# Smallest score chunks first for the first pair, products of zeros ahead of it, and new durations and numbers in the plan of a mixer kernel

## The chip, the core and the metric

The kernel runs on one core of a Trainium2 chip. The metric is the device time in microseconds (us) of one execution, lower is better. Three runs of the kernel before took 779.51, 781.88 and 781.61 us; their median is 781.61 us. The trace read below is of one further, profiled execution.

## The reference

`B, H, S, D = 4, 12, 448, 64`, `DM = 768`. Causal attention per head is followed by a two-stage mixer (tokens, then channels) with residuals and by a gated block whose gate is mixed over tokens after a layer normalisation.

```python
scores = q @ k.T / 8, masked above the diagonal
attn = exp(scores - max) / (sum + 1e-9)
x = (attn @ v), heads joined                       # (4, 448, 768)
h = relu(x^T @ w_tok1) @ w_tok2                    # over tokens
u = x + h^T
x = u + relu(u @ w_ch1) @ w_ch2                    # over channels, 1536 wide
h = relu(x @ w_in); u, v = halves of h             # 512 each
v_n = (v - mean(v)) / sqrt(var(v) + 1e-6)
out = (u * (w_spatial @ v_n + b_spatial)) @ w_out
```

## The kernel before, in words

All of it is one program of four batches. Products that need full precision are made of three products of rounded parts: a value is split into a high part (a copy to the shorter type, by ACT) and a low part (value minus high part, `lo_part` at line 251, by DVE or POOL), and `mm3` (line 257) multiplies high by high, high by low and low by high.

**Attention.** 24 pairs of heads go through `scores` (line 360), `transposed` or `turned` (lines 460 and 505) and `weighted` (line 556). A pair's scores are computed in four chunks of query rows (64, 128, 128 and 128 rows against 64, 192, 320 and 448 keys), two heads side by side, into four PSUM banks. Pairs below `WHOLE` multiply the loaded values (tile `stage`) directly; later pairs are first split by `split_qk` (line 348; tiles `qh`, `ql`). DVE adds the mask and finds the row extreme (line 417), ACT takes the exponentials and their sums (line 434), DVE adds 1e-9 to the eight sums and inverts them (lines 442 and 443), POOL scales (line 451). Pairs below `BLOCKS` are transposed on PE in 16 blocks (line 488), copied out of PSUM (lines 492 and 494) and multiplied with the values `v` (lines 592 and 597). Later pairs are transposed by DVE (line 518) and through DRAM by SP's transfers, and multiplied at line 578. Pairs below `AHEAD` use four places for their scores, later ones two.

**Mixers.** `token_mix` works per half batch (tiles `xs`, `hid`, sums into `U` at line 695). `channel` (line 769) does batches 0 and 1 with weights `whl` (tiles `uhl`, `hid`, sums at line 767); `channel_pair` (line 947) does batches 2 and 3 together with seven products in place of eight (`factors` at line 802, `split_weights` at line 838, `seven` at line 915; PSUM tiles `psf`, operands `fb` and `fa`, sums at lines 908 and 987). Weights arrive in double precision and DVE narrows them in three operations (lines 276, 278 and 280: tiles `way` and `gw`).

**Gated block.** For batches 0 and 1 and then 2 and 3 the first half of the hidden channels is again made by seven products (`hidden_pair`, line 1158), the other half by `value` (line 1077): 18 products into `psv`, a ReLU by ACT into one of two buffers `v` (line 1096), statistics by DVE (`first`, lines 1099 to 1101), a square root by ACT (line 1104), and normalisation by DVE (`second`, lines 1108 to 1113, output `vn`). `spatial` (line 1253) multiplies with `w_spatial` (PSUM `psp`), DVE adds the bias (line 1269) and multiplies by the gate (line 1270). `out_factors` and `project` (lines 1195 and 1281) make the output.

**The order.** Nothing is issued as it is written. Each piece is a `job` with an engine, a duration in us, what it reads and writes, and a priority; `Plan.order` (line 126) runs a list schedule over all jobs with those durations, and the instructions of each engine are emitted in the order of the planned start times. Each engine then executes its list in order. Jobs marked `port` and all POOL jobs exclude each other in the plan. A PSUM bank is chosen in the plan as well: the one that came free last, where one is free. So a wrong duration puts work in an order, or a tile in a bank, that does not suit the real times. Lines that the steps below touch:

```python
job("DVE", 0.8, first, r=[(v, 0)], w=[st], prio=p0)                  # line 1103
job("DVE", 0.65, second, r=[st, (v, 0)], w=[st, dkey], prio=p0)      # line 1115
v = buf(f"p{turns[0] % 2}", [FF], F32, "v")                          # line 1088
s = max(s, min(bank_free[i] for i in b.banks))                       # line 154
```

Of the kernel before, what the change touches and what calls it, by code (L numbers as in the profile page):

```python
# [9 lines left out]
F32 = mybir.dt.float32  # L10
# [25 lines left out]

DIRECT = tuple(range(3))

WHOLE = 6

AHEAD = 11

EAGER, START, STEP = 12, 110.0, 16.7

LO_DVE = tuple(range(7))
WEIGHT_LO_DVE = tuple(range(7))

GATE_DVE = tuple(range(8))
OUT_DVE = tuple(range(7))

VALUE_DVE = ()
NORMED_DVE = (1, 2, 3)

EARLY = 1e5 + 48
VALUE_PRIO = -1e5 + 1.5

GATED = 6.0, 0.3
GATED_AT = 160.0, 5.0

MOVE = 0  # L60
WEIGHT_PRIO = -0.7

AHEAD_OF_USE = 9.0
LEAD, SLOPE = 14.0, 2.0

BLOCKS = 16


class Buf:
# [20 lines left out]
class Plan:  # L90
# [11 lines left out]
    def job(self, eng, us, emit, r=(), w=(), touch=(), prio=0.0, at=0.0, size=0, port=False):  # L102


        j = Job(eng, us, emit, prio, at, size, len(self.jobs), port)
        for k in r:
            if k in self.writer:
                j.before.add(self.writer[k])
            self.readers.setdefault(k, []).append(j)
        for k in w:  # L110
            if k in self.writer:
                j.before.add(self.writer[k])
            j.before.update(self.readers.get(k, ()))
            self.writer[k] = j
            self.readers[k] = []
        j.before.discard(j)
        for k in (*r, *w):
            if isinstance(k[0], Buf):
                j.bufs.add(k[0])
        for b in j.bufs:  # L120
            b.jobs.append(j)
        j.bufs |= set(touch)
        self.jobs.append(j)
        return j
# [79 lines left out]
def mixer_kernel(ctx: ExitStack, tc: tile.TileContext, qkv, wtok, wch, wgv, wsp, bsp, out):  # L204
# [126 lines left out]
    def load(n):  # L331
        st = stage[n % 2]
        operands[n] = {"st": st}
        p = n - 2.0
        src = qkv[n // NP, n % NP]
        job("SP", 0.4, lambda: nc.sync.dma_start(st.t, src[:, : 2 * S]), w=[(st, 0)], prio=p, size=458752)
        v = buf(f"v{n % 2}", [8, D], F32, "v")
        operands[n]["v"] = v
        job("SP", 0.4, lambda: nc.sync.dma_start(v.t, src[:, 2 * S :].rearrange("p (c d) -> p c d", d=D)), w=[(v, 0)], prio=p + 0.1, size=262144)

    def prio_of(n):

# [17 lines left out]
    def scores(n):  # L360
# [35 lines left out]
        def ps(i, j):  # L396
            k, o_ = PLACE[i]
            M, W = CHUNKS[i][1] - CHUNKS[i][0], CHUNKS[i][1]
            return banks[j][k].t[:M, o_ : o_ + W]

        def mms():
            for i in (3, 0, 2, 1):
                q0, q1 = CHUNKS[i]
                W = q1
                ks = [slice(2 * S - W, 2 * S) if n < BLOCKS else slice(S, S + W), slice(S, S + W)]
                for k, (a, c) in enumerate(terms):
                    for j in range(2):
                        r = slice(64 * j, 64 * j + 64)
                        nc.tensor.matmul(ps(i, j), a.t[r, q0:q1], c.t[r, ks[j]], start=(k == 0), stop=(k == last))  # L409

        pkeys = [(banks[j][k], 0) for j in range(2) for k in range(2)]
        job("PE", 2.5 if whole else 1.95, mms, r=split_keys, w=[*pkeys, ("scored", n)], touch=holds, prio=n, at=nominal(n))
        for i in (3, 0, 2, 1):
            M, W = CHUNKS[i][1] - CHUNKS[i][0], CHUNKS[i][1]
            for j in range(2):
                def ttr(i=i, j=j, M=M, W=W):
                    nc.vector.tensor_tensor_reduce(  # L417
                        out=P(i)[:M, j, :],
                        in0=ps(i, j),
                        in1=mask[:M, S - 128 : S - 128 + W] if j == 0 and n < BLOCKS or M == 64 else mask[:M, S - W : S],  # L420
                        scale=-1.0 / 8.0,
                        scalar=3.0e38,
                        op0=ALU.add,
                        op1=ALU.min,
                        accum_out=s.t[:M, 0, 2 * i + j : 2 * i + j + 1],
                    )

                job("DVE", (W * 1.06 + 65) / 1e3, ttr, r=[(banks[j][PLACE[i][0]], 0), MASK], w=[pk(i, j), (s, "nm", i, j)], prio=prio_of(n))
        for i in (3, 0, 2, 1):
            M, W = CHUNKS[i][1] - CHUNKS[i][0], CHUNKS[i][1]  # L430
            for j in range(2):
                def ex(i=i, j=j, M=M):
                    c = 2 * i + j
                    nc.scalar.activation(  # L434
                        P(i)[:M, j, :], P(i)[:M, j, :], AF.Exp, bias=s.t[:M, 0, c : c + 1], scale=-1.0, accum_out=s.t[:M, 1, c : c + 1]
                    )

                job("ACT", (W * 0.833 + 279) / 1e3, ex, r=[(s, "nm", i, j), pk(i, j)], w=[pk(i, j), (s, "sum", i, j)], prio=prio_of(n))
# [638 lines left out]
    def value(lhs, keys, key, dst, dkey):  # L1077
# [22 lines left out]
            nc.vector.bn_aggr(sc(6, 2), sc(0, 6))  # L1100
            nc.vector.tensor_scalar_add(sc(8), sc(7), LN_EPS)

        job("DVE", 0.8, first, r=[(v, 0)], w=[st], prio=p0)
        job("ACT", 0.25, lambda: nc.scalar.activation(sc(9), sc(8), AF.Sqrt), r=[st], w=[st], prio=p0)

        def second():
# [5 lines left out]
            nc.vector.tensor_scalar_mul(r, r, t)  # L1112
            nc.vector.tensor_scalar(dst(), v.t, sc(6), r, op0=ALU.subtract, op1=ALU.mult)

        job("DVE", 0.65, second, r=[st, (v, 0)], w=[st, dkey], prio=p0)
        normal[key] = dst, dkey

    def gate_unit(f):
# [198 lines left out]
    project(1, place, ws, (1, 2))  # L1317


    make_identity(nc, ident)  # L1320
    nc.gpsimd.memset(mask, 0.0)
    diag = mask[:, S - 128 : S]
# [2 lines left out]
    )  # L1325
    for s in stats:
        nc.gpsimd.memset(s.t, 0.0)
    for t in small:

        nc.gpsimd.memset(t.t[64:128, 384:512], 0.0)  # L1330
    for j in plan.order():
        j.emit()
    mctx.__exit__(None, None, None)
# [69 lines left out]
```

## Time and profile before

| | |
|---|---|
| median of three runs | 781.61 us |
| profiled execution, own time | 780.77 us |
| its span, first to last instruction | 779.0 us |
| PE busy | 747.1 us (96%) |
| DVE busy | 637.7 us (82%) |
| ACT busy | 432.7 us (56%) |
| POOL busy | 259.8 us (33%) |
| mean granted clock of TensorE | 0.989 |

PE is the engine with the most work, so the time is read as PE's work plus the stretches in which PE has nothing to do. A busy PE can still be slow: the granted clock of a stretch tells whether it ran at the higher or the lower of its two levels.

### The profile page before, as it was taken

Reading aid. Unit: us, or ns where it says so; the run is one execution under the profiler, and the core shown is the slowest. Engines: PE = TensorE matmul, PEld = TensorE weight load, DVE = VectorE, ACT = ScalarE, POOL = GpSimd, SP = SyncE. Lnnn points to the kernel's source line nnn. Section 1 sums busy time; section 2 is a strip of 40 time slices with the busy share of each in tenths; the row PEclk is TensorE's granted clock in tenths of the full one; section 3 lists DMA queues with packets and bytes.
Section 4 is the critical chain, followed back from the end, with each engine's and each line's share of the span. In section 5 each row is a group of like instructions: output and inputs, shape, how many; then the busy total and the mean of one; then the engine's idle time right before and its main releaser. Section 6 shows DMA issues by size and latency. Waiting matters only on the chain.

```text
span 779.0 us, 12423 instructions
## 1 busy us (share of the span) xinstructions
PE 747.1 (96%) x4200; PEld 640.8 (82%) x4200; DVE 637.7 (82%) x1528; ACT 432.7 (56%) x1049; POOL 259.8 (33%) x333
## 2 busy tenths in 40 slices
PE   6889899999999999999998999999998999989998
PEld 3467678888988788888887999998887888879997
DVE  5899878898877868787479879999999797689582
ACT  5999766644455665542345667454554655535241
POOL 4789646375856564652500000001310200200000
PEclk9999999999999999999999999999999999989999
DMA  7677585789857998988732212322301100300113
GB/s 263 212 241 245 196 310 201 233 293 315 282 174 229 298 300 251 279 254 259 200 122 111 68 56 82 130 93 82 96 0 41 41 1 18 112 0 36 72 48 130
DMA packets 49679, 124.11 MB, mean 159 GB/s; under 512 B 4944, under 2 KB 20944, under 8 KB 49104
## 3 DMA queue, kind: packets, MB, share of 16 engines
q1 hardware_dynamic: 49616, 123.33, 48.3%
q8 instruction: 33, 0.54, 0.3%
q14 instruction: 30, 0.25, 0.1%
HBM read 92.50 MB, written 30.80 MB: 158 GB/s over the span
## 4 chain that ended last, share of the span: by engine, by line
PE 61%; DVE 27%; ACT 6%; issue 3%; DMA 2%; POOL 1%; DVEq 0%; ACTq 0%; POOLq 0%; SPq 0%
PE ps L261 7%; PE ps L263 7%; PE ps L262 7%; DVE fb L252 6%; PE psf L261 5%; PE psf L263 5%; PE psf L262 5%; DVE fa L252 4%; PE pss L409 4%; DVE raw L859 3%; PE pst L488 3%; DVE U L987 2%; PE pso L578 2%; ACT P L434 2%; DVE U L815 2%
## 5 line engine op out<-in xcount | busy, mean ns | idle before, releaser
L261 PE MATMUL psf<-fb,fa 128*128 128x448 f32 x420 | 154.7, 368 | 4.4 <-DVE hs L908 1.6
L263 PE MATMUL psf<-fb,fa 128*128 128x448 f32 x420 | 154.0, 367 | 0.0
L262 PE MATMUL psf<-fb,fa 128*128 128x448 f32 x420 | 154.0, 367 | 0.0
L252 POOL TENSOR_TENSOR whl<-whl 128x768 fp32r<-128x768 f32 x45 | 83.5, 1859 | 88.3 <-ACT whl L727 80.2
L451 POOL TENSOR_SCALAR P<-P,stats 128x448 f32<-128x448 f32 (+1 forms) x192 | 88.0, 477 | 48.4 <-DVE stats L443 36.3
L434 ACT ACTIVATE P<-P,stats 128x448 f32<-128x448 f32 (+1 forms) x192 | 95.9, 506 | 10.9 <-DVE stats L417 10.7
L261 PEld LDWEIGHTS psf<-fb,fa 128*128 128x128 f32 x420 | 79.3, 189 | 13.4 <-issue 1.9
L262 PEld LDWEIGHTS psf<-fb,fa 128*128 128x128 f32 x420 | 79.3, 189 | 6.7
L263 PEld LDWEIGHTS psf<-fb,fa 128*128 128x128 f32 x420 | 79.2, 189 | 6.8 <-DVE fa L252 0.2
L417 DVE CUSTOM_DVE_ANT_0 P<-pss,mask 128x448 f32<-128x448 f32 (+1 forms) x192 | 68.8, 412 | 15.0 <-PE pss L409 14.9
L846 ACT CAST fa<-raw 128x384 fp32r<-128x384 f32 (+1 forms) x112 | 57.0, 531 | 41.4 <-DVE raw L859 18.4
L252 DVE TENSOR_TENSOR fa<-raw,fa 128x384 fp32r<-128x384 f32 (+1 forms) x112 | 65.5, 611 | 9.8 <-ACT fa L846 9.6
L727 ACT CAST whl<-whl 128x768 fp32r<-128x768 f32 x45 | 37.2, 832 | 52.1 <-DMA whl<-plain 50.5
L252 POOL TENSOR_TENSOR wv<-wf,wv 128x512 fp32r<-128x512 f32 x6 | 8.5, 1430 | 161.0 <-DVE fb L252 153.1
L261 PE MATMUL ps<-uhl,whl 128*128 128x448 f32 x144 | 55.2, 383 | 0.0
L261 PE MATMUL ps<-hid,whl 128*128 128x448 f32 x144 | 54.2, 377 | 0.6 <-DVE U L767 0.6
L263 PE MATMUL ps<-hid,whl 128*128 128x448 f32 x144 | 52.7, 366 | 0.0
L263 PE MATMUL ps<-uhl,whl 128*128 128x448 f32 x144 | 52.7, 366 | 0.0
L262 PE MATMUL ps<-hid,whl 128*128 128x448 f32 x144 | 52.7, 366 | 0.0
L262 PE MATMUL ps<-uhl,whl 128*128 128x448 f32 x144 | 52.6, 365 | 0.0
L810 ACT CAST fb<-U 128x448 fp32r<-128x448 f32 x57 | 30.2, 566 | 29.5 <-DVE U L815 12.2
L488 PE MATMUL pst<-ident,P 128*128 128x128 f32 x256 | 38.7, 287 | 5.7 <-POOL P L451 4.5
(163 smaller groups left out, 1772.9 us busy)
## 6 DMA issues: line engine op xcount, KB each, us to landing
way<-in_wch SPq DMA_DIRECT2D x24, 768.0 KB, 6.1
whl<-plain SPq DMA_DIRECT2D x45, 384.0 KB, 5.4
stage<-in_qkv SPq DMA_DIRECT2D x24, 448.0 KB, 4.3
plain<-way SPq DMA_DIRECT2D x24, 384.0 KB, 3.8
raw<-plain SPq DMA_DIRECT2D x24, 384.0 KB, 3.7
round<-PB SPq DMA_DIRECT2D x8, 1024.0 KB, 6.8
PT<-round SPq DMA_DIRECT2D x32, 256.0 KB, 7.1
v<-in_qkv SPq DMA_DIRECT2D x24, 256.0 KB, 4.5
```

The costliest lines, as they stand in the source:

```text
L252: e.tensor_tensor(lo, x, hi.bitcast(F32), op=ALU.subtract)
L261: nc.tensor.matmul(ps, ah, bh, start=(first and i == 0), stop=False, **kw)
L262: nc.tensor.matmul(ps, ah, bl, start=False, stop=False, **kw)
L263: nc.tensor.matmul(ps, al, bh, start=False, stop=(last and i == n - 1), **kw)
L409: nc.tensor.matmul(ps(i, j), a.t[r, q0:q1], c.t[r, ks[j]], start=(k == 0), stop=(k == last))
L417: nc.vector.tensor_tensor_reduce(out=P(i)[:M, j, :], in0=ps(i, j), in1=mask[:M, S - 128 : S - 128 + W] if j == 0 and n < BLOCKS or M == 64 ...
L434: nc.scalar.activation(P(i)[:M, j, :], P(i)[:M, j, :], AF.Exp, bias=s.t[:M, 0, c : c + 1], scale=-1.0, accum_out=s.t[:M, 1, c : c + 1])
L451: nc.gpsimd.tensor_scalar(P(i)[:M, j, :], P(i)[:M, j, :], s.t[:M, 2, c : c + 1], 1.0, op0=ALU.mult, op1=ALU.mult)
L488: nc.tensor.transpose(ps.t[:, c : c + 128], src, ident)
L727: job("ACT", act(DM, False), lambda: nc.scalar.copy(w.t[:, 0, :], w.t[:, 1, :].bitcast(F32)), r=ks, w=ks, prio=p)
L810: job("ACT", act(S, False), lambda: nc.scalar.copy(f(0), x_()), r=wk, w=[(h, k, 0)], prio=p)
L846: job("ACT", act(n, False), lambda: nc.scalar.copy(part(o, 0), at(d)), r=[key(d)], w=[wk], prio=p + 0.1 * o)
```

## The change

The first pair's chunks are computed and read in the order 64, 192, 320, 448 keys instead of 448, 64, 320, 192; its `v` is loaded after the second pair's `stage`. DVE clears a buffer first of all and PE multiplies zeros by zeros (448 and 256 columns) into a PSUM bank that nothing reads. The plan gets 1.0 and 1.45 us for the two DVE parts of a value's statistics. Besides, its numbers change: one more pair (number 6) multiplies unsplit (`WHOLE`), pair 10 uses two places instead of four (`AHEAD`), pair 16 is transposed on PE instead of DVE and DRAM (`BLOCKS`), the low parts of product 0 of the gated block go from DVE to POOL (`GATE_DVE`), the splits of the value weights `wv` get a late priority (`VALUE_PRIO`), and several start times and priorities move.

```diff
-WHOLE = 6
-AHEAD = 11
-EAGER, START, STEP = 12, 110.0, 16.7
+WHOLE = 7
+AHEAD = 10
+EAGER, START, STEP = 12, 105.0, 16.4
-GATE_DVE = tuple(range(8))
+GATE_DVE = (1, 2, 3, 4, 5, 6, 7)
-EARLY = 1e5 + 48
-VALUE_PRIO = -1e5 + 1.5
+EARLY = 1e5 + 40
+VALUE_PRIO = 100.0
-GATED_AT = 160.0, 5.0
+GATED_AT = 160.0, 7.0
-AHEAD_OF_USE = 9.0
-LEAD, SLOPE = 14.0, 2.0
-BLOCKS = 16
+AHEAD_OF_USE = 12.0
+LEAD, SLOPE = 12.0, 2.0
+BLOCKS = 17
...
-        job("SP", 0.4, lambda: nc.sync.dma_start(v.t, src[:, 2 * S :].rearrange("p (c d) -> p c d", d=D)), w=[(v, 0)], prio=p + 0.1, size=262144)
+        job("SP", 0.4, lambda: nc.sync.dma_start(v.t, src[:, 2 * S :].rearrange("p (c d) -> p c d", d=D)), w=[(v, 0)], prio=p + (0.1 if n else 1.1), size=262144)
...
+        chunks = (3, 0, 2, 1) if n else range(4)
+
         def mms():
-            for i in (3, 0, 2, 1):
+            for i in chunks:
...
-        for i in (3, 0, 2, 1):
+        for i in chunks:
...
-        job("DVE", 0.8, first, r=[(v, 0)], w=[st], prio=p0)
+        job("DVE", 1.0, first, r=[(v, 0)], w=[st], prio=p0)
...
-        job("DVE", 0.65, second, r=[st, (v, 0)], w=[st, dkey], prio=p0)
+        job("DVE", 1.45, second, r=[st, (v, 0)], w=[st, dkey], prio=p0)
...
+    nc.vector.memset(small[0].t, 0.0)
+    zeros = psp.tile([128, 512], F32, tag="b7", name="zeros")
+    for n in (S, 256):
+        nc.tensor.matmul(zeros[:, :n], small[0].t[:, :128], small[0].t[:, :n], start=True, stop=True)
...
-    for t in small:
-
-        nc.gpsimd.memset(t.t[64:128, 384:512], 0.0)
+
+    nc.gpsimd.memset(small[1].t[64:128, 384:512], 0.0)
```

How instructions move is shown at three places, all on DVE, whose list PE waits for there.

**Place A**, the end of the first pair's score chunks and its inversion of sums (`way_149` and `way_152` are the first token weights, `stats_65` holds the first pair's sums). Before, and then in the change:

```order
L417 ISA P_69,stats_65<-pss,mask 128x192
L417 ISA stats_65 128x1
L276 TENSOR_SCALAR psw<-way_149 128x384
L278 SCALAR_TENSOR_TENSOR psw<-way_149,psw 128x384
L280 SCALAR_TENSOR_TENSOR way_149<-way_149,psw 128x384
L442 TENSOR_SCALAR stats_65<-stats_65 128x8
L443 RECIPROCAL stats_65<-stats_65 128x8
```

```order
L419 ISA P_177,stats_65<-pss,mask 128x448
L419 ISA stats_65 128x1
L276 TENSOR_SCALAR psw<-way_152 128x384
L278 SCALAR_TENSOR_TENSOR psw<-way_152,psw 128x384
L280 SCALAR_TENSOR_TENSOR way_152<-way_152,psw 128x384
L444 TENSOR_SCALAR stats_65<-stats_65 128x8
L445 RECIPROCAL stats_65<-stats_65 128x8
```

The last chunk is now the one of 448 keys; the narrowing of the first weights still stands ahead of the inversion.

**Place B**, the statistics of the first values of batches 0 and 1 (`U_5599` and `U_5474` are the fetched activations that `factors` subtracts and splits). Before, and then in the change:

```order
L815 TENSOR_TENSOR U_5599<-U_5599 128x448
L1099 BN_STATS bias<-v 128x6
L1100 BN_AGGR bias<-bias 128x2
L1101 TENSOR_SCALAR bias<-bias 128x1
L1099 BN_STATS bias<-v 128x6
L1100 BN_AGGR bias<-bias 128x2
L1101 TENSOR_SCALAR bias<-bias 128x1
L1108 RECIPROCAL bias<-bias 128x1
L1110 TENSOR_SCALAR bias<-bias 128x1
L1111 TENSOR_SCALAR bias<-bias 128x1
L1112 TENSOR_SCALAR bias<-bias 128x1
L1113 TENSOR_SCALAR vn<-v,bias 128x512
```

```order
L989 TENSOR_TENSOR U_2484<-psf,U_2484 128x448
L1101 BN_STATS bias<-v 128x6
L1102 BN_AGGR bias<-bias 128x2
L1103 TENSOR_SCALAR bias<-bias 128x1
L252 TENSOR_TENSOR fb<-U_5474,fb 128x448
L817 TENSOR_TENSOR U_5444<-U_5444 128x448 x3
L252 TENSOR_TENSOR fb<-U_5444,fb 128x448 x2
L252 TENSOR_TENSOR fb<-U_5474,fb 128x448
L817 TENSOR_TENSOR U_5474<-U_5474 128x448
L252 TENSOR_TENSOR fb<-U_5444,fb 128x448
L252 TENSOR_TENSOR fb<-U_5474,fb 128x448 x2
L817 TENSOR_TENSOR U_5474<-U_5474 128x448
```

The first value's statistics stood behind nearly all subtractions and splits of `U`; now they stand right behind the last sum of the channel mixer, with some of those splits between their two parts.

**Place C**, the last value's statistics and the first bias additions of `spatial` (`fa<-raw` and `raw<-raw` are the output weights' splits and sums, `gate_6375` and `gate_6304` the gate of batch 0). Before, and then in the change:

```order
L252 TENSOR_TENSOR fa<-raw,fa 128x768
L1099 BN_STATS bias<-v 128x6
L1100 BN_AGGR bias<-bias 128x2
L1101 TENSOR_SCALAR bias<-bias 128x1
L252 TENSOR_TENSOR fa<-raw,fa 128x768
L1269 TENSOR_TENSOR psp<-psp,bias 128x448
L1108 RECIPROCAL bias<-bias 128x1
L1110 TENSOR_SCALAR bias<-bias 128x1
L1111 TENSOR_SCALAR bias<-bias 128x1
L1112 TENSOR_SCALAR bias<-bias 128x1
L1113 TENSOR_SCALAR vn<-v,bias 128x512
L1270 TENSOR_TENSOR gate_6375<-psp,gate_6375 128x448
```

```order
L1101 BN_STATS bias<-v 128x6
L1102 BN_AGGR bias<-bias 128x2
L1103 TENSOR_SCALAR bias<-bias 128x1
L861 TENSOR_TENSOR raw<-raw 128x768
L1110 RECIPROCAL bias<-bias 128x1
L1112 TENSOR_SCALAR bias<-bias 128x1
L1113 TENSOR_SCALAR bias<-bias 128x1
L1114 TENSOR_SCALAR bias<-bias 128x1
L1115 TENSOR_SCALAR vn<-v,bias 128x512
L1271 TENSOR_TENSOR psp<-psp,bias 128x448
L1272 TENSOR_TENSOR gate_6304<-psp,gate_6304 128x448
L1271 TENSOR_TENSOR psp<-psp,bias 128x448
```

Splits of the output weights have moved from ahead of the first bias addition to behind the first two pairs of bias and gate operations.

## Rows read from the trace of the kernel before

**Rows 1.** Four stretches: us; busy PE, PE loads, DVE, ACT, POOL; granted clock, DMA.

```profile
0.00:100.00 100.00, 83.75 (x579) 57.73 (x580) 84.94 (x296) 82.09 (x254) 72.71 (x131) 0.97 0.70 234
100.00:400.00 300.00, 298.79 (x1897) 256.54 (x1896) 232.03 (x598) 153.85 (x381) 163.49 (x169) 1.00 0.80 255
...
540.00:600.00 60.00, 56.22 (x255) 48.33 (x254) 58.92 (x115) 31.03 (x71) 13.71 (x18) 0.97 0.19 58
600.00:700.00 100.00, 96.39 (x441) 84.39 (x440) 81.50 (x183) 54.01 (x119) 9.93 (x16) 0.97 0.11 34
```

**Rows 2.** Waits of PE: total us, times, longest us.

```profile
PE psp L1262 <- DVE gate L1270: 3.3, 1, 3.3
PE psv L261 <- ACT v L1096: 2.7, 2, 2.4
...
PE psf L261 <- ACT wv L1063: 1.3, 1, 1.3
PE psm L649 <- DVE xs L252: 1.3, 1, 1.3
```

**Rows 3.** PE's busy time and granted clock (the number behind the bracket), single microseconds.

```profile
80.00:81.00 1.00, 1.00 (x7) 0.50 0.45 174
...
83.00:84.00 1.00, 1.00 (x10) 0.80 0.74 215
...
589.00:590.00 1.00, 1.00 (x4) 0.50 0.00 0
...
697.00:698.00 1.00, 1.00 (x4) 0.60 0.00 0
```

**Rows 4.** The chain that ended last, pieces on PE: start us, us, what.

```profile
33.75 2.28 PE pss L409 x16
...
109.92 1.78 PE pss L409 x24
111.70 0.90 PE pso L592 x4
112.61 1.30 PE pso L597 x12
113.90 0.59 PE pst L488 x4
...
271.18 2.21 PE pso L578 x24
```

**Rows 5.** The chain from 0 to 60 us, three pieces.

```profile
3.99 4.33 PE pss L409 x16
...
9.76 0.52 DVE psw L276
...
42.99 0.83 ACT qh L354
```

**Rows 6.** Timeline of the first 30 us: SP's issue of the token weights, DVE's inversion.

```profile
2.58 1.51 SPq L306 DMA_DIRECT2D way<-in_wtok  x3
...
11.57 0.20 DVE L443 RECIPROCAL stats<-stats 128x8 f32<-128x8 f32 x1
```

**Rows 7.** Transfers: the first token weights, KB, us from issue to landing.

```profile
way<-in_wtok SPq DMA_DIRECT2D x1, 768.0 KB, 7.1
```

**Rows 8.** Timeline of DVE at one value's statistics.

```profile
681.41 0.69 DVE L1099 BATCH_NORM_STATS2 bias<-v 128x6 f32<-128x512 f32 x1
...
684.69 0.95 DVE L252 TENSOR_TENSOR fa<-raw,fa 128x768 fp32r<-128x768 f32 x1
685.56 0.69 DVE L1099 BATCH_NORM_STATS2 bias<-v 128x6 f32<-128x512 f32 x1
```

**Rows 9.** Timeline at 553 us: a split on DVE beside one on POOL.

```profile
552.97 1.30 POOL L252 TENSOR_TENSOR wv<-wf,wv 128x512 fp32r<-128x512 f32 x1 [3.80 <-ACT wv L1063]
```

**Rows 10.** Timeline of DVE, the same split beside that one, and alone.

```profile
551.62 0.55 DVE L252 TENSOR_TENSOR fa<-raw,fa 128x384 fp32r<-128x384 f32 x1
...
553.09 1.59 DVE L252 TENSOR_TENSOR fa<-raw,fa 128x384 fp32r<-128x384 f32 x1
```

More of the change, by code (lines that the diff above doesn't have):

```diff
@@ L428, in scores @@
                 job("DVE", (W * 1.06 + 65) / 1e3, ttr, r=[(banks[j][PLACE[i][0]], 0), MASK], w=[pk(i, j), (s, "nm", i, j)], prio=prio_of(n))
-        for i in (3, 0, 2, 1):
+        for i in chunks:
             M, W = CHUNKS[i][1] - CHUNKS[i][0], CHUNKS[i][1]
```

## The prediction

> **What bounds the kernel now.** I read the busy times by stretch first, then PE's waits, then the clock, then the chain of work that ended last.
>
> PE has the most work. In the stretch from 100 to 400 us it is busy for 298.8 of 300 us: there only PE's own work counts, and whatever is added to it lengthens the run [rows 1]. Elsewhere PE stands idle: 16.2 us before 100 us, 3.8 us between 540 and 600 and 3.6 us between 600 and 700 [rows 1]. DVE is busy for 58.9 of 60 us in the first of these two late stretches and for 81.5 of 100 in the second. So late in the run PE waits for an engine that is full at the time.
>
> The waits name the places [rows 2]. The longest is 3.3 us at the first products of `spatial` (line 1262), for the gate operation that empties a PSUM bank (line 1270). Next come 2.7 us, 2.4 of it at once, at the value products, for a ReLU by ACT (line 1096). That ReLU writes one of only two buffers `v`, so for the third value it needs the first one's normalisation by DVE to be over. Two waits of 1.3 us follow: one for the `wv` splits near 546 us, one for the `xs` splits near 79 us.
>
> A long wait costs more than its length. After each of these three places the granted clock is 0.50, the lower of TensorE's two levels, 1.2 GHz [rows 3]. It is below 1 from 80.0 to 83.4 us (first and last of four such rows), for 3.4 us around 589 us (one of four), and from the restart at 692.1 to 697.8 us (last of six). At half the rate half of such a time is lost: 1.7, 1.7 and 2.8 us.
>
> **The change part by part.** The sum is made on the profiled execution, 780.77 us, which is 0.84 us under the median of 781.61 us.
>
> 1. *Work added on PE: +2.9.* Pair 16 is now transposed on PE. Four transposes take 0.59 us there, so its 16 take 2.36 us; its products with `v` take 0.90 + 1.30 = 2.20 us in that form, and 2.21 us in the one that they leave [rows 4]. Pair 6 is now multiplied unsplit: 2.28 us in place of 1.78, so 0.50 more [rows 4]. Sum 2.86 us. Pair 16 stands in the stretch without idle time, so nothing hides it. The DVE transposes and SP's five transfers that it saves (one out, four back) were hidden.
>
> 2. *Zeros and the first pair's order: 0.* The first pair's 16 score records take 4.33 us, against 2.28 us for the same records of a later pair [rows 4, 5]: they run at the lower level, although the page's clock column shows full speed there. With zeros multiplied before 3.99 us, while the `stage` transfer is awaited, and with the small chunks first, DVE and ACT should be done with this pair up to 2.05 us sooner. But the next thing on DVE's list is the narrowing of the first token weights, and only behind it stands the inversion of sums, for which POOL's scaling and then PE's transposes wait; place A shows this order unchanged. That transfer is issued at 2.58 us [rows 6] and lands 7.1 us later [rows 7], at 9.68 us, and the narrowing starts at 9.76 [rows 5]. The same bytes are issued ahead of it as before, only in another order. So the inversion should stay near 11.57 us [rows 6] and the gain end there as idle time on DVE. Bounds: -2.05 if the weights land that much sooner, +0.3 if the zeros run past the landing of `stage`. I take 0.
>
>    The Trainium skill ("TensorE: Matmul & The Clock Gate", the section on the clock gate) says that the throttled state is the default and that activity releases it. The slow rows of the first pair agree. By that rule alone the zeros would give the whole 2.05 us; by the order at place A they give none, and the order decides what I take.
>
> 3. *The early gap: -2.8.* Without pair 6's split, ACT saves a cast of 0.83 us that stands on the chain [rows 5]. Pair 10 now uses the two shared places and its scores come later on all lists. Before, DVE read them just ahead of the `xs` split for which PE waited 1.3 us, and the first channel products (`uhl`) stood on PE behind that wait. Now that split comes sooner, and six of these products stand on PE earlier. I take 0.8 + 1.3, and 0.7 of the 1.7 us lost to the clock, since other engines also hold the chain there. Bounds: 0 (the gap moves to another pair) and -3.8.
>
> 4. *Statistics of the values: -3.5 at place B, -5.5 at place C.* Between the start of one value's statistics and the next free moment, with one split of 0.87 us taken off (684.69 to 685.56), DVE spends 684.69 - 681.41 - 0.87 = 2.41 us [rows 8]. The plan allowed 0.8 + 0.65 = 1.45 us; it now allows 2.45. Each value put DVE 1 us behind its plan, 14 values in all, and both late waits lie where several values come in a row. At place B the first value's statistics now stand right behind the last channel sum and no longer behind the subtractions; at most 2.4 + 1.7 = 4.1 us goes. At place C three splits of 0.87 us leave the list ahead of the first bias operation and one more leaves from between the first two gate operations: the second of these, which lets PE go on, comes 3.5 us sooner, more than the 3.3 us of wait. With the clock, 3.3 + 2.8 = 6.1 us can go. I take a little less than either and bound both by 0, if other waits appear in their stead. Behind place C the splits that moved are needed by the output products only some 18 us later (88 products of `spatial` at 0.2 us), so that DVE has time for them.
>
> 5. *The `wv` splits: -0.6.* They now come behind the last splits that the channel mixer needs. Half of the 1.3 us; bounds 0 and -1.3.
>
> 6. *Low parts moved to POOL: +1.5.* Six splits of 448 and three of 384 columns leave DVE and go to POOL. A split on DVE took 1.59 us while POOL ran one of 1.30 us, against 0.55 us alone, so 1.04 us more [rows 9, 10]. Nine such delays make 9.4 us, and DVE saves nine times 0.55, 5.0 us: 4.4 us more for DVE. Between 600 and 700 us it has 18.5 us to spare, between 540 and 600 only 1.1 [rows 1]. Three of the nine fall into the latter: 3 x 0.5. Bounds 0 and +4.4.
>
> 7. *New small waits: +1.0.* Every list is rearranged. The waits not named above are mostly 0.3 to 0.7 us; I allow for two more. Bounds 0 and +3.
>
> Sum: 2.9 + 0 - 2.8 - 3.5 - 5.5 - 0.6 + 1.5 + 1.0 = -7.0 us; 780.8 - 7.0 + 0.8 = 774.6, **774.5 us**.
>
> **The rivals.**
>
> *The start counts too.* If the first token weights land sooner, or the inversion follows at once, the 2.05 us of step 2 are kept: 772.5 us. For it: every later pair follows the first one. Against it: place A. Chance 0.12.
>
> *POOL takes back what DVE gained.* The Trainium skill ("SBUF — State Buffer", the section with the doors' diagram) calls the pair of ports shared by DVE and GpSimd an exclusive lock: the one that comes second waits for the whole of the other's instruction. The 1.04 us extra beside a POOL split of 1.30 us agree. As a mechanism here: the splits on POOL fall into the stretch in which DVE has 1.1 us to spare, all 4.4 us lie on the path (2.9 more than in step 6), and the first value's statistics come late again (3.5 us lost): 774.5 + 6.4 = 780.9 us, no change. Against it: the plan keeps POOL and DVE apart, and only three of the nine come so early. Chance 0.16.
>
> *Slower: pairs 10 to 12 come late.* Their inversions stand 13 us of DVE's work or more further down its list, counted with durations of these rows' kinds, while PE's list asks for pair 10's transposes only about 5 us of its own work later. If DVE and then POOL are not done when PE arrives, PE waits as near 79 us, 1.3 us and 1.7 us for the clock, once for each of the three pairs: 9.0 us, and the 2.0 us of that gap are not won. 774.5 + 11.0 = 785.5 us. It decides if pair 10's scaling ends after PE reaches its transposes; PE's longer early list and POOL's shorter one (no split of pair 6) speak against it. Chance 0.12.
>
> **How the numbers follow.** The forecast has 0.60; its own range is 770 to 778.5. About 0.3% of the median, 2.3 us, is what a measurement of this kernel can tell from no change: faster means under 779.3, slower over 783.9. Forecast and first rival are faster, 0.72, and of the second rival's 0.16 some 0.03 falls under 779.3 as well: 0.75. Same 0.13, slower 0.12. The range of 769.5 to 781.0 holds the forecast, the first rival down to the point where steps 3 to 5 give a little more, and the second rival; it leaves out the third and the far ends of the bounds.
>
> **What would show it.** In the new profile: no wait of PE at lines 1264 and 1098 above 1 us and no low clock near 590 and 690 us (step 4); the reciprocal of the first pair still near 11.5 us, with DVE idle before the first narrowing, and the first pair's records near 3 us instead of 4.33 (step 2); less than 14 us of idle time of PE before 100 us (step 3); 272 transposes in place of 256 (step 1); splits on DVE of more than 1 us beside POOL between 560 and 640 us (step 6). The forecast is wrong if PE's idle time after 400 us is still above 10 us, or if new waits for POOL's scaling stand between 90 and 160 us.

## The result and the profile after

The change takes 767.85 us (median of four runs, 766.64 to 769.46) where the kernel before took 780.56 in the same comparison: a ratio of 0.985, interval 0.981 to 0.989. It is faster, as forecast, but the time lies 1.65 us under the range, and 12.7 us were gained where the forecast from the median shown was 7.1. Run again beside three of the experiments, the change took 770.04 us (six runs, 766.49 to 777.07; ratio 0.987, 0.983 to 0.991). Over all ten runs its median is 768.85 us, which is the measure below, called 769.

The profiled execution took 769.46 us with a span of 767.7, that is 11.3 us less than the one before (780.77 and 779.0). The four stretches of [rows 1] in the profile of the change, same columns:

```profile
0.00:100.00 100.00, 85.72 (x574) 58.72 (x575) 83.06 (x284) 79.05 (x240) 67.62 (x121) 0.98 0.73 248
100.00:400.00 300.00, 298.43 (x1908) 256.73 (x1908) 229.12 (x608) 156.61 (x398) 165.97 (x176) 1.00 0.77 245
540.00:600.00 60.00, 58.34 (x271) 50.13 (x270) 59.02 (x114) 31.19 (x73) 19.27 (x22) 1.00 0.19 57
600.00:700.00 100.00, 100.00 (x473) 87.99 (x472) 84.94 (x189) 57.46 (x124) 13.80 (x20) 1.00 0.11 34
```

PE's idle time fell from 16.2 to 14.3 us before 100 us, from 3.8 to 1.7 between 540 and 600 and from 3.6 to nothing between 600 and 700; the clock column of both late stretches is full. Before 100 us, though, 2.72 us of the busy time are now the zeros (row shown under "The start"): without them PE stood idle for 17.0 us there, more than before. The waits of PE behind 500 us, against [rows 2]:

```profile
PE psf L261 <- ACT fa L848: 0.7, 1, 0.7
PE psf L261 <- DVE U L989: 0.4, 1, 0.4
PE psv L261 <- ACT v L1098: 0.3, 1, 0.3
PE psf L261 <- ACT v L1098: 0.2, 1, 0.2
```

Places B and C are gone, and so is the lower clock behind each. To see where the time went, each execution is cut at two marks of PE's list: the first product into `psf` (start of the paired channel mixer) and the first into `psp` (start of `spatial`). The three stretches before, then in the change, with the columns of [rows 1]:

```profile
0.00:409.50 409.50, 390.75 (x2513) 321.43 (x2513) 326.21 (x911) 242.86 (x649) 236.20 (x299) 0.99 0.76 245
409.50:682.02 272.52, 266.51 (x1261) 237.10 (x1261) 244.43 (x496) 154.99 (x335) 23.64 (x34) 0.99 0.20 67
682.02:775.08 93.06, 89.81 (x429) 82.25 (x427) 67.02 (x123) 34.28 (x65) 0.00 (x0) 0.96 0.15 55
```

```profile
0.00:407.36 407.36, 391.51 (x2516) 322.13 (x2517) 319.47 (x904) 240.53 (x647) 233.59 (x296) 1.00 0.75 241
407.36:676.65 269.29, 266.21 (x1262) 235.77 (x1260) 242.64 (x492) 157.03 (x338) 34.97 (x43) 1.00 0.20 67
676.65:763.98 87.33, 87.33 (x429) 79.97 (x427) 67.11 (x119) 34.22 (x65) 0.00 (x0) 1.00 0.16 59
```

The first stretch is 2.1 us shorter, the middle one (with place B) 3.2, the last one (with place C) 5.7, and the end behind it 0.2.

### The profile page after: what moved, and what is told of

It is laid out like the page before. It is cut to its first block, busy times and chain, and to the rows that moved or that the text cites. A ratio compares the mean times of both kernels' runs of the same rounds, so it can differ in the third digit from the quotient of the medians.

```text
span 767.7 us, 12418 instructions
## 1 busy us (share of the span) xinstructions
PE 745.0 (97%) x4204; PEld 637.9 (83%) x4204; DVE 629.2 (82%) x1513; ACT 432.3 (56%) x1050; POOL 268.6 (35%) x339
## 4 chain that ended last, share of the span: by engine, by line
PE 71%; DVE 18%; ACT 5%; DMA 3%; issue 1%; POOL 1%; SPq 0%; DVEq 0%; ACTq 0%
PE psf L261 8%; PE psf L263 8%; PE psf L262 8%; PE ps L261 7%; PE ps L263 7%; PE ps L262 7%; PE pss L411 4%; DVE fb L252 3%; DVE fa L252 3%; ACT P L436 3%; PE pst L490 2%; DVE U L989 2%; PE pso L580 2%; DVE raw L861 2%; PE psm L261 2%; PE psm L263 2%
## 5 line engine op out<-in xcount | busy, mean ns | idle before, releaser
L436 ACT ACTIVATE P<-P,stats 128x320 f32<-128x320 f32 (+2 forms) x192 | 96.0, 506 | 7.7 <-DVE stats L419 7.6
L419 DVE CUSTOM_DVE_ANT_0 P<-pss,mask 128x320 f32<-128x320 f32 (+2 forms) x192 | 69.4, 413 | 14.3 <-PE pss L411 13.6
L252 POOL TENSOR_TENSOR fb<-U,fb 128x448 fp32r<-128x448 f32 x6 | 7.6, 1296 | 147.8 <-ACT fb L812 147.8
```

The lines of the kernel that those rows point to most:

```text
L252: e.tensor_tensor(lo, x, hi.bitcast(F32), op=ALU.subtract)
L419: nc.vector.tensor_tensor_reduce(out=P(i)[:M, j, :], in0=ps(i, j), in1=mask[:M, S - 128 : S - 128 + W] if j == 0 and n < BLOCKS or M == 64 ...
L436: nc.scalar.activation(P(i)[:M, j, :], P(i)[:M, j, :], AF.Exp, bias=s.t[:M, 0, c : c + 1], scale=-1.0, accum_out=s.t[:M, 1, c : c + 1])
```

## Experiments

Sixteen runs, in four groups; the kernels of a group ran on the same chip. Ratios are to the kernel before, which took 780.2 to 781.1 us in each group. The change itself ran again beside the f runs only; the others are set against its 768.85 us across chips.

### The durations, the splits on POOL, the zeros

**e1.** The kernel before with the two durations alone.

```diff
-job("DVE", 0.8, first, ...)
+job("DVE", 1.0, first, ...)
-job("DVE", 0.65, second, ...)
+job("DVE", 1.45, second, ...)
```

> The kernel before with the two new durations (1.0 and 1.45 us) alone. Its list shows the second gate operation of place C as in the change, but place B nearly as before: the first value's statistics still stand behind the subtractions, and the first normalisation even comes 12 rows further behind them. Theory (durations give place C, the gated block's moved splits give place B): the wait of 3.3 us before line 1262 and the 2.8 us of low clock behind it are gone, -6; place B keeps its wait or lengthens it, 0 to +3: 775 to 778 us where the kernel before takes 780.6. Rival (the durations give both places, as the prediction has it): both waits gone, -9 to -10, 771 us. Rival (neither: the numbers of the plan do it): 780 us.

Measured: 772.66 us, ratio 0.990 (0.988 to 0.992). **e2**, the change with these two lines undone.

> The change with the old durations 0.8 and 0.65 us. Only the lists behind some 560 us differ from the change. Theory: place C comes back whole, a wait of about 3 us of PE before line 1264 and low clock behind it, +5.5 to +6: 773.5 us where the change takes 768; place B stays without a wait. Rival (other moves opened place C): within 1 us of the change. Rival (durations also opened place B): both waits back, +9 to +10, 777 us.

Measured: 777.32 us, ratio 0.997 (0.995 to 0.998). Both medians are nearer to the prediction's step 4, which stood there as the rival with 771 and 777. By the medians two numbers in the plan are worth 8.1 us on the kernel before and 8.5 on the change. The traces agree with the rival in e1, where the wait for line 1096 is gone, and not wholly in e2: its profiled execution, 775.39 us, has a span 5.9 us longer than the change's, of which 4.9 are in the last stretch and 1.5 in the middle one. There PE waits 1.5 us for a ReLU (line 1098) and 1.1 us for a gate's sum at the full clock, so that place B comes back in part only; no trace shows what makes the median another 1.9 us higher. The middle stretch, first e1, then e2:

```profile
408.79:679.58 270.79, 266.20 (x1260) 237.20 (x1261) 243.75 (x500) 155.41 (x336) 30.49 (x34) 0.99 0.20 67
```

```profile
406.86:677.63 270.77, 264.75 (x1262) 235.67 (x1260) 242.17 (x488) 156.22 (x337) 40.10 (x43) 1.00 0.20 67
```

The last stretch shows place C by itself, first e1, then e2:

```profile
679.58:766.91 87.33, 87.33 (x429) 79.97 (x427) 67.11 (x119) 34.17 (x65) 0.00 (x0) 1.00 0.15 58
```

```profile
677.63:769.87 92.24, 88.99 (x429) 81.35 (x427) 66.91 (x123) 34.29 (x65) 0.00 (x0) 0.98 0.15 56
...
689.00:690.00 1.00, 1.00 (x4) 0.91 (x3) 0.97 (x3) 0.00 (x0) 0.00 (x0) 0.50 0.00 0
```

With the new durations the stretch takes 87.33 us to the hundredth in e1 and in the change; with the old ones the lower clock is back (the second row), and ahead of it the wait, from the list of PE's waits in e2:

```profile
PE psp L1264 <- DVE gate L1272: 3.3, 1, 3.3
```

At place B e1 has no wait for line 1096, although DVE's list there still has the first value's statistics behind the subtractions. What changed is PE's own list. The value products (`psv`) in stretches, before and in e1 (us, busy PE, count, clock):

```profile
566.00:589.40 23.40, 19.03 (x78) 0.98 0.00 0
589.40:598.00 8.60, 0.32 (x2) 0.85 0.33 93
```

```profile
567.00:585.60 18.60, 16.51 (x72) 1.00 0.00 0
585.60:598.20 12.60, 0.21 (x1) 1.00 0.21 64
598.20:601.00 2.80, 2.72 (x12) 1.00 0.00 0
```

A value is 18 products. Before, PE's list asked for 78 of them, four values and a third of the fifth, ahead of the next long run of other work, and the fifth had to wait for a ReLU (line 1096, [rows 2]). In e1 it asks for 72, then does 54 products of the gate, and the fifth value comes after 12.6 us without a value product, when its bank is free. Presumably the plan, told that statistics take longer, no longer counted on that bank; this is read from the lists, and no run isolates it. In e1 the middle stretch still has a wait of 1.9 us for a sum at line 987 near 547 us with 3.4 us of lower clock behind it, which the change does not have. It stands where PE waited for the `wv` splits before, and with it the middle stretch of e1 is only 1.7 us shorter than before (270.79 us against 272.52).

**e3.** The change with one line as before:

```diff
-GATE_DVE = (1, 2, 3, 4, 5, 6, 7)
+GATE_DVE = tuple(range(8))
```

> The change with the low parts of product 0 of the gated block on DVE again, none of these nine on POOL. Theory (this move opened place B, since it takes nine splits out of DVE's full stretch): the first value's statistics stand behind the subtractions again, PE waits 2 to 5 us at line 1098 and runs at the low clock for 3.4 us, +4 to +6: 772 to 774 us. Rival (the prediction's step 6: POOL's splits slow DVE's down by 1.04 us each): without them DVE gains up to 4.4 us, 0 to -1.5: 766.5 to 768 us.

Measured: 769.76 us, ratio 0.986 (0.984 to 0.989): the change itself, within what can be told. Both expectations fell. The statistics stand behind the subtractions again and PE waits for no ReLU, as in e1; and nine splits less on POOL make nothing faster. The equal times are not equal traces, though. In e3 PE waits 1.8 us for a sum near 544 us, and the lower clock follows for 3.4 us; there the change waits 0.7 us for a split and keeps its clock. Elsewhere between the marks e3 makes that up, 269.6 us against 269.3 (PE's waits in e3, and one microsecond of its stretches):

```profile
PE psf L261 <- DVE U L989: 1.8, 1, 1.8
```

```profile
544.00:545.00 1.00, 1.00 (x4) 0.50 0.00 0
```

POOL's splits do hold DVE up in the change: two splits of 384 columns beside three of POOL's took 2.41 us, where two such took 1.02 in the profile before (at 540.83 us). The timeline of the change:

```profile
538.11 4.21 POOL L252 TENSOR_TENSOR fb<-U,fb 128x448 fp32r<-128x448 f32 x3 [147.82 <-ACT fb L812]
...
540.32 2.41 DVE L252 TENSOR_TENSOR fa<-raw,fa 128x384 fp32r<-128x384 f32 x2
```

But between the two marks DVE is busy for 244.04 us in e3 and for 242.64 in the change, with nine splits less. At 0.55 us each these nine are 5.0 us, of which 1.4 are saved; so the delays cost about 3.6 us (an estimate from these figures), 0.4 us for each split on POOL.

**e4.** The change without the zeros.

```diff
-    zeros = psp.tile([128, 512], F32, tag="b7", name="zeros")
-    for n in (S, 256):
-        nc.tensor.matmul(zeros[:, :n], small[0].t[:, :128], small[0].t[:, :n], start=True, stop=True)
```

> The change without the two products of zeros (the clearing of the buffer stays); every list is otherwise the same. Theory: the first pair's records take 4.2 to 4.4 us at the lower clock instead of 2.76; with the chunk of 448 keys last, both halves of each bank are complete only at the end, so DVE's first read moves from 7.0 to about 8.5 us and the inversion from 11.6 to about 13.0: +1.4, 769.5 us. Rival (the first weights' narrowing sets the inversion, as the prediction has it): the inversion stays within 0.3 us of 11.6 and the time within 0.3 us of the change.

Measured: 771.19 us, ratio 0.988 (0.986 to 0.990). The order of events is the theory's: DVE reads first at 7.95 us and inverts at 12.56, 0.9 us later than in the change. The time is higher by about as much as these intervals can tell.

### The start

**f1** is the change once more.

> The change itself once more, as the measure for the three kernels beside it. Both theories: 767 to 770 us, a ratio of 0.984 to 0.987 to the kernel before.

Measured: 770.04 us (above). **f2**, the change with the old chunk order:

```diff
-chunks = (3, 0, 2, 1) if n else range(4)
+chunks = (3, 0, 2, 1)
```

> The change with the first pair's chunks in the old order (448, 64, 320, 192 keys), zeros kept. Theory (chunks of 448 and 64 keys share a PSUM bank, so with the small ones first no bank is complete before the last record, and this gave back what the zeros won): DVE's first read moves from 7.0 to about 5.7 us and its last ends near 8.5 instead of 9.9; then the narrowing waits for its weights, which land near 9.5 us, so the inversion moves only from 11.6 to about 11.3: 0 to -0.4, within 0.4 us of the change. Rival (small chunks first is what helps): the inversion comes later and the time is 1 us longer.

Measured: 770.15 us, ratio 0.987 (0.984 to 0.989). **f3** undoes this, the zeros and the order of the loads:

```diff
-    zeros = psp.tile([128, 512], F32, tag="b7", name="zeros")
...
-chunks = (3, 0, 2, 1) if n else range(4)
+chunks = (3, 0, 2, 1)
...
-prio=p + (0.1 if n else 1.1)
+prio=p + 0.1
```

> The change without the zeros, with the old chunk order and the old order of the first loads; all later lists as in the change. Theory (the prediction's step 2, the whole start is worth nothing): the inversion stays at 11.5 to 11.7 us and the time within 0.5 us of the change, 768 to 769 us. Rival (the start is worth the 2.4 us that the kernel without zeros lost): 770.5 us.

Measured: 770.43 us, ratio 0.986 (0.983 to 0.989), with the inversion at 11.86 us. **f4** has the old chunk order and the zeros, and emits the first narrowing behind the inversion and the second behind the second pair's reads:

```diff
-    for j in plan.order():
+    jobs = plan.order()
+    late = set(narrowed[:3])
...
+    jobs[a : z + 1] = [j for j in jobs[a : z + 1] if j not in late] + [j for j in jobs[a : z + 1] if j in late]
...
+    for j in jobs:
```

> The change with the old chunk order, zeros kept, and DVE's list rearranged: the first pair's inversion stands ahead of the first narrowing, the second narrowing behind the second pair's reads (its cast on ACT behind that pair's exponentials). Theory (the narrowing in front of the inversion is what held the start back): the inversion moves from 11.6 to about 10.4 us, POOL's scaling and PE's transposes 1.2 us sooner, of which 0.5 to 1.2 us are kept: 767 to 767.5 us. Rival (ACT, busy 38 of 40 us behind 20 us, or the first clock episode sets the pace anyway): within 0.3 us of the kernel with the old chunk order.

Measured: 769.28 us, ratio 0.986 (0.983 to 0.988). The inversion came at 11.04 us, held now by ACT's exponentials (timeline of DVE):

```profile
10.83 0.17 DVE L446 TENSOR_SCALAR stats<-stats 128x8 f32<-128x8 f32 x1 [1.91 <-ACT P L438]
11.04 0.20 DVE L447 RECIPROCAL stats<-stats 128x8 f32<-128x8 f32 x1
```

All four are one time: the whole start is worth nothing that can be measured, and an inversion 0.6 us sooner neither. Each of these times is known to 2 or 3 us only, so that they do not rule out a gain of 2 us; the argument against one is the inversion, which none of the four brought ahead of 11.04 us. The change's start shows why. PE's zeros and first records, then DVE's first read, the narrowing and the inversion, from its timeline:

```profile
1.45 2.72 PE L1325 MATMUL zeros<-P 128*128 128x448 f32 x4 [1.45 <-DVE P L1322]
4.18 2.71 PE L411 MATMUL pss<-stage 64*64 64x64 f32 x16
...
7.03 0.22 DVE L419 CUSTOM_DVE_ANT_0 P<-pss,mask 64x64 f32<-64x64 f32 x1 [5.64 <-PE pss L411]
...
9.79 0.55 DVE L276 TENSOR_SCALAR psw<-way 128x384 uint32<-128x384 uint32 x1
...
11.64 0.20 DVE L445 RECIPROCAL stats<-stats 128x8 f32<-128x8 f32 x1
```

The records are 1.6 us shorter than the 4.33 of [rows 5]. But the chunks of 64 and 448 keys share a PSUM bank (one tile of the program), and DVE's first read waited for the last record, so it came at 7.03 us; before, with the bank of the first two chunks complete half way, it came at 6.41. DVE's reads end at 9.86 us in place of 9.75. One part of the start took what the other gave, and the narrowing stands behind both.

The zeros also do not do the same in each execution. The same program in f1:

```profile
4.27 3.88 PE L411 MATMUL pss<-stage 64*64 64x64 f32 x16
...
8.29 0.22 DVE L419 CUSTOM_DVE_ANT_0 P<-pss,mask 64x64 f32<-64x64 f32 x1 [6.90 <-PE pss L411]
...
12.90 0.20 DVE L445 RECIPROCAL stats<-stats 128x8 f32<-128x8 f32 x1
```

### The numbers of the plan, one by one

Each run is the change with one line as it was.

```diff
-BLOCKS = 17
+BLOCKS = 16
```

> The change with pair 16 transposed by DVE and DRAM again; all lists up to about 250 us are the same. Theory (its transposes on PE are work in a stretch without idle time, and nothing else comes of it): 1.7 to 2.4 us less PE work, so 1.7 to 2.4 us faster than the change, 766.5 to 767 us where the change takes about 769. Rival (the relief of DVE's and SP's lists by this pair pays for it elsewhere): within 0.5 us of the change, or slower, with new waits of PE for DVE or DMA behind 250 us.

**g1** measured: 769.98 us, ratio 0.985 (0.982 to 0.987): no gain from the work taken off PE. Its profiled execution, the slowest of the five with 773.11 us, shows where it can have come back, at 421 to 427 us, where the paired channel mixer begins and PE waits for a sum by DVE, with the lower clock behind it (PE's waits in g1, and one microsecond of its stretches):

```profile
PE psf L261 <- DVE hs L910: 2.9, 1, 2.9
```

```profile
424.00:425.00 1.00, 1.00 (x4) 0.90 (x3) 0.96 (x3) 0.21 (x1) 0.00 (x0) 0.50 0.00 0
```

The change waits there for 1.4 us and keeps its clock. I call it place D below.

```diff
-WHOLE = 7
+WHOLE = 6
```

> The change with pair 6 split again. Theory (the prediction's step 3 by its parts): a cast of 0.83 us more on ACT's chain before 59 us, 0.5 us less PE work: +0.3 against the change, 769.3 us. Rival (this split made the gap near 79 us): PE waits over 1.2 us there and falls to the low clock, +2 to +2.5, 771 us.

**g2** measured: 768.13 us, ratio 0.983 (0.980 to 0.985): pair 6 unsplit is worth nothing, perhaps less.

```diff
-AHEAD = 10
+AHEAD = 11
```

> The change with four places for pair 10 as well. Theory (the gap near 79 us was opened by this): the first channel products start at about 98 us instead of 85, PE waits and loses clock near 80 us as in the kernel before, +1.5 to +3 against the change: 770.5 to 772 us. Rival (the low clock near 80 us falls or not by itself, since the change still waits 1 us there): within 0.5 us of the change.

**g3** measured: 779.49 us, ratio 0.998 (0.997 to 1.000): 10.6 us slower than the change, more than any expectation. The profiled execution has its `psf` mark at 415.5 us, 8.1 later than the change's. PE was idle for 3.25 us between 100 and 120 us, where the change lost 0.24; first g3, then the change:

```profile
100.00:120.00 20.00, 16.75 (x120) 11.89 (x119) 13.61 (x37) 11.80 (x32) 4.81 (x5) 1.00 0.67 227
```

```profile
100.00:120.00 20.00, 19.76 (x143) 15.80 (x143) 16.87 (x44) 14.56 (x37) 9.88 (x13) 1.00 0.76 249
```

Between 100 and 400 us g3 lost 6.3 us in all, the change 1.6 here, but 4.8 in f1's execution, whose `psf` mark came at 414.9 us. So the traces show a part of the 10.6 us at most.

```diff
-EAGER, START, STEP = 12, 105.0, 16.4
+EAGER, START, STEP = 12, 110.0, 16.7
```

> The change with the old start times of the later pairs (110 and 16.7 in place of 105 and 16.4). Theory (these numbers only move scores inside the stretch from 100 to 400 us where PE is never idle): within 0.5 us of the change. Rival (they closed the waits of 0.3 to 1.3 us between 240 and 440 us): PE idle time between 100 and 440 us rises by 1 to 2 us, 770 to 771 us.

**g4** measured: 773.35 us, ratio 0.989 (0.987 to 0.991), 4.5 us slower by the medians, though its interval overlaps those of the change. The profiled execution, the fastest of its six, took 769.39 us, as the change's did, with a wait of 2.9 us at place D and no lower clock behind it; so this wait is not shown to be what costs the 4.5 us. `START` also does more than my expectation says: in the plan (line 195 of the kernel before) a result of another engine is taken to reach PE another 0.3 us later before that time, and 0.8 us later from it on.

### Together

**h1** undoes the places of pair 10 and the start times, both:

```diff
-AHEAD = 10
+AHEAD = 11
-EAGER, START, STEP = 12, 105.0, 16.4
+EAGER, START, STEP = 12, 110.0, 16.7
```

> The change with four places for pair 10 and with the old start times (110, 16.7), both undone together. Theory (the two belong together: each setting of the places has start times that suit it, and as a pair they are worth the early gain of 2 to 3 us): 771 to 772 us where the change takes about 769. Rival (the places of pair 10 are worth the 10 us that the run with them alone lost): 778 us or more. Rival (they are worth nothing as a pair): 769 us.

Measured: 775.22 us, ratio 0.995 (0.993 to 0.997). **h2** adds both to e1's kernel:

```diff
-AHEAD = 11
+AHEAD = 10
-EAGER, START, STEP = 12, 110.0, 16.7
+EAGER, START, STEP = 12, 105.0, 16.4
```

> The kernel before with the new durations, two places for pair 10 and the new start times. Theory (an early gain of 2 to 3 us on its own): first channel products near 85 us in place of 98, 769.5 to 770.5 us where the new durations alone take 772.7. Rival (these numbers suit only the whole set): 772 us or more, with new waits of PE between 100 and 250 us.

Measured: 771.91 us, ratio 0.990 (0.988 to 0.992). **h3** adds pair 16 on PE to e1's kernel:

```diff
-BLOCKS = 16
+BLOCKS = 17
```

> The kernel before with the new durations and pair 16 transposed on PE. Theory (the work on PE is paid in full in a stretch without idle time, as the prediction has it): 1.7 to 2.4 us slower than the new durations alone, 774.5 to 775 us. Rival (as the run of the change with pair 16 back on DVE suggests, DVE's and SP's relief closes waits behind 400 us that are worth as much): 771.5 to 773 us, with less than 1 us of idle time of PE between 400 and 440 us.

Measured: 776.24 us, ratio 0.995 (0.993 to 0.997). In the change the two numbers together are worth 6.4 us, on e1's kernel 0.75, within the intervals; pair 16 on PE costs 3.6 us on e1's kernel and nothing in the change. So pair 16 is paid on e1's kernel and made up for in the change; which of the change's other numbers do this was not tested. PE's waits at place D differ in these runs: waits of 2.1 us in h1 and 2.9 in h2, both with the lower clock behind, and in h3 seven waits of 0.2 to 1.1 us between 422 and 438 us, 4.3 in all; e1 waits 1.6 and the change 1.4. From PE's timeline in h1:

```profile
425.54 0.44 PE L261 MATMUL psf<-fb,fa 128*128 128x448 f32 x1 [2.13 <-DVE hs L910]
```

**h4** is f4 with pair 6 split:

```diff
-WHOLE = 7
+WHOLE = 6
```

> The change with pair 6 split again, the old chunk order, zeros kept, and the first pair's inversion ahead of the first narrowing. Theory (0.7 us from the first, 0.5 us from the others, as their runs had it): 767 to 768 us, a ratio of 0.981 to 0.984 to the kernel before. Rival (both differences were within what the start of the run varies by): as the change, 769 us.

Measured: 769.28 us, ratio 0.986 (0.984 to 0.989). The rival holds: I found no kernel that beats the change by more than the measurement tells.

## Why the prediction fell short

The direction and the largest term were right. The sum of -7.0 should have been -11.3 on the profiled executions; another 2.4 us lie between these and the medians (0.84 that I added, and the 1.6 by which the change's profiled execution is above the median of its first four runs).

- **Step 4, durations: -9.0 forecast, -8.1 and -8.5 measured by the medians (e1, e2).** Place C is right in place, cause and size: -5.5 forecast, 5.7 in the last stretch. At place B the wait went as forecast, but the cause was wrong: I read the first value's statistics as the key and the durations as what moved them. e1 and e3 have them behind the subtractions and no wait for the ReLU. The durations acted through PE's list. The -3.5 of place B is not shown by itself: the middle stretch is 1.7 us shorter in e1 than before, and 1.5 us shorter in the change than in e2. That the whole came so near to -9.0 is in part luck.
- **Step 2, the start: 0 forecast, nothing that can be told from 0 measured (without it f3 is 0.4 us above f1).** The inversion went from 11.57 to 11.64 us, in the range of steps that I named. But I wrote that DVE would be idle ahead of the narrowing; it was not, since I had taken both parts of the start as gains and did not ask when a bank is complete. The zeros shortened the first pair's records by 1.6 us in one execution and by 0.45 in another of the same program, and not by the whole 2.05, and nothing of it shows in the time. That activity releases the throttled state is what the Trainium skill says ("TensorE: Matmul & The Clock Gate", the section on the clock gate); these two traces agree with it in part.
- **Step 3, the early gap: -2.8 forecast.** Its two parts were wrong. Pair 6 gives nothing (g2). The `xs` wait near 79 us is still there, 1.0 us in place of 1.3; what went is the lower clock behind it, in this execution, and with it 1.7 us where I took 0.7. PE's idle time before 100 us did not fall under the 14 us that I named as the sign: it is 14.3, and 17.0 without the zeros. The places of pair 10 are worth 10.6 us as the one thing undone and 6.4 with the start times undone as well: no sum of waits near 79 us contains that.
- **Step 1, work on PE: +2.9 forecast (its terms make 2.85), about 1.4 measured as work and none of it in the time.** Ahead of the `psf` mark PE was busy for 390.75 us before and is for 391.51 in the change. Take off the 2.72 us of zeros, and put back the 1.6 us by which the first pair's records are shorter and the 1.7 us that the lower clock near 80 us cost: some 1.4 us of work were added (an estimate from these rows). The pst group, before and after, grew by 0.8 us for 16 more transposes, partly since four of the earlier ones had run at the lower clock near 80 us:

```profile
L488 PE MATMUL pst<-ident,P 128*128 128x128 f32 x256 | 38.7, 287 | 5.7 <-POOL P L451 4.5 <-ACT PT L494 0.7 <-ACT U L600 0.3
```

```profile
L490 PE MATMUL pst<-ident,P 128*128 128x128 f32 x272 | 39.5, 281 | 6.0 <-POOL P L453 3.0 <-DVE hid L255 1.1 <-ACT PT L496 1.1
```

  The sentence that failed is "nothing hides it". Before, PE did stand idle between pair 16's stretch and the mark: for 1.1 us between 200 and 400 us, and for 1.3 us at 409.5 us, where it waited for a sum by DVE. The change has neither. With pair 16 back on DVE (g1) PE stands idle for 1.7 us between 200 and 400 us, against 0 to 1.0 in the runs that have it on PE and the rest as in the change or nearly so, and longer at place D; the wait at 409.5 us does not come back there, so another number closed it. My list of waits had passed over the one at 409.5 us and place D's 1.6 us. The first of them, in the kernel before:

```profile
PE psf L261 <- DVE U L767: 1.3, 1, 1.3
```

- **Step 6, POOL: +1.5 forecast, 0 measured within what can be told (e3).** The delay of DVE beside POOL is real. The Trainium skill ("SBUF — State Buffer", the section with the doors' diagram) and the trace agree on it (2.41 us for two splits of 0.5). But I charged nine delays of 1.04 us, and the change set against e3 puts them at about 0.4: the moved splits leave DVE with 1.4 us less to do between the marks, not with 4.4 more.
- **Step 7, new waits: +1.0 forecast, nothing as a sum measured.** Behind 500 us the new ones are 0.2 to 0.7 us, and the old ones they replace were longer. Ahead of 140 us two new ones did come, 1.1 us at 93 us and 1.3 us at 129, but others closed, as step 1 tells. Step 5's wait (1.3 us for `wv`) is gone as said, with 0.7 at `fa` in its stead; it is gone in e1 too, where the priority of these splits is the old one, so that the new priority is not shown to have done it.

By stretch: forecast +0.1, measured -2.1 before `psf`; forecast -2.6 (B, `wv` and POOL), measured -3.2 between the marks; forecast -5.5, measured -5.7 behind `psp`; the +1.0 of step 7 nowhere. The step that failed is the charging of steps 1, 6 and 7, 5.4 us together, at full price in a kernel whose plan re-sorts everything around them. In their place the runs showed 1.4 us of added work, against which stand 2.4 us of waits that closed (not all of them through pair 16), a move to POOL that takes time off DVE, and new waits no longer than those that went. Of the rivals none came: pairs 10 to 12 are not late, and POOL took nothing back.

Not settled: why the places of pair 10 and the start times, undone one at a time, cost 10.6 and 4.5 us and both together 6.4. The traces show idle time at other places in each (100 to 120 us in g3, place D in g1, g4, h1 and h2), but what in the lists decides it was not isolated. The change is 3.8 us faster than e1, and of this no run gives the parts: `EARLY`, `VALUE_PRIO`, `GATED_AT`, `AHEAD_OF_USE` and `LEAD` were never undone by themselves.

## What to carry to other kernels

In a kernel whose order comes from a plan, a duration that is planned 1 us too short can be worth 8 us of 780, as here: compare the plan's durations with the trace first, and look for the effect in the list of the engine that waits, not only of the one that was mis-timed. Do not add up the plan's numbers: undo them one by one and in pairs, since here 10.6, 4.5 and 6.4 us stood for the same two. Before smaller pieces are put first, ask which bank they share and when it is complete.

## What was not expected of the hardware

The same program, on the same chip, took 766.49 to 777.07 us in six runs. The profiled one, the slowest, had the lower granted clock from 11.7 to 21.7 us, where the change's first profile, behind the same wait of 2.5 us for DVE's reads, had it for 3.4 us from 15.7; and once more at 134 to 138 us. Its `psf` mark came 7.5 us later than in the first profile, 5.1 of them by the clock (half of the 10.2 us more at the lower level); behind the mark the two agree to 0.1 us. So a difference of some us ahead of that mark, between single profiles, shows little. Two microseconds of f1:

```profile
13.00:14.00 1.00, 1.00 (x8) 0.69 (x10) 0.97 (x3) 0.33 (x1) 0.68 (x2) 0.50 0.05 22
...
135.00:136.00 1.00, 1.00 (x4) 1.00 (x4) 0.50 (x2) 1.00 (x5) 0.00 (x0) 0.50 0.50 54
```

Likewise the wait of 1.0 to 1.3 us near 80 us is followed by the lower clock before and in e3, h2 and h3, and in none of the fourteen other profiles. That a given wait costs the clock as well is not certain in these runs: I had counted on each clock loss going with its wait.
